# Splitting a weight conversion into two calls, reordering GpSimd's two operations on it, and finishing tiles one further ahead

## The chip, the core and the metric

The kernel runs on one core of one Trainium2 chip. The metric is device microseconds of one execution. TensorE (PE) does matmuls, VectorE (DVE), ScalarE (ACT) and GpSimd (POOL) do elementwise work, and SyncE's queue (SP) issues every DMA. Each engine works through its own instructions in the order in which they stand in the program.

## The reference

A retention layer over 4 batches, 8 heads, 768 positions and head size 64, followed by two feed-forward layers over 3072 tokens:

```
state = gamma * state + outer(k_t, v_t);  y_t = scale * q_t @ state
x = y as 3072 x 512
x = leaky_relu(x @ w1_in) @ w1_out            # 512 -> 2048 -> 512
x = h * sigmoid(1.702 h) @ w2_out, h = x @ w2_in
```

The four weights arrive as 64-bit floats, two 32-bit words for each element, and the kernel turns them into 32-bit floats by integer operations on the chip.

## The kernel before, in words

**Precision.** Each feed-forward product is made of three TensorE passes: an operand is split into a rounded part `hi` (ACT, L62) and a remainder `lo` (L63, on DVE, or on POOL for weights), and the passes are hi by lo, hi by hi, lo by hi, in this order. A weight tile of 128x512 thus needs `hi` for the first two matmuls of a group of 12 and `lo` from the third on.

**Converting a weight tile.** A weight has 16 tiles (index m). `load_raw` (L65) brings a raw tile (buffer "raw", 3 of them). `convert` (L70) does two ACT operations (L76 absolute value of the high word into tile "a", of which there are 2; L77 scaling of the low word), four DVE operations (L78, L79, L81 with one input, L83 with two) and one POOL addition (L85). `finish` (L88) then splits "a" into `hi` (ACT, L62) and `lo` (POOL, L63). For the second layer `finish_away` (L95) does the same and stores the result to DRAM, from where it is loaded again later.

**The schedule.** Three stages matter here; their names are used below.
- Stage A: 24 retention steps s (loop at L290 to L312). A step issues to PE the scores of s+1 (L200), the state and output matmuls of s (L231, L237, L243), then, on 15 of the steps 5 to 22 and on step 4, one group of 12 feed-forward matmuls `ffn_in(0, 0, m)` (L148). Steps 8, 13, 18 and 23 have no group. DVE does the masked scores "sm" (L204), the state "st" (L246) and "qs" (L211), POOL does "ks" (L215), SP loads the input of step s+4 into one of four buffers (L190).
- Stage B: the outer loop i = 16 to 25 at the end of the function. `out_of(n)` for n = 0 to 15 does the first block's output groups (L329, 12 matmuls each) and, between them, the input groups of the second block. Index i=16 has one output group, i=17 to 22 have two each, i=23 to 25 one each; each i has one input group before them. `out_of` issues the output group, then splits the activations of the group after next (`g_split`: ACT L62, DVE L63, into one of 2 tiles "g"), then calls `work()`.
- Stage C: everything after. `stage2` (L353) converts the second layer's weights there.

`work()` (L129) is called once for each tile of the first layer's 32: call n starts the load of tile n+2, converts tile n, and finishes tile n-1. The calls stand at steps 2, 3, 5, 6, 7, 8, 10, ... of stage A (L298), then once before the loop of stage B (L375) and once in each `out_of` of stage B. So the group for tile m is issued to PE right after the `work()` that finishes tile m (stage A), or in the `out_of` after it (stage B), and the POOL queue reads: addition of tile n, remainder of tile n-1.

Of the kernel before, what the change touches and what calls it, by code (L numbers as in the profile page):

```python
# [13 lines left out]
I32 = mybir.dt.int32  # L14
AF = mybir.ActivationFunctionType
ALU = mybir.AluOpType
# [8 lines left out]
KF = DFF // P  # L25
# [16 lines left out]
def retention_two_ffn(ctx: ExitStack, tc: tile.TileContext, qkv, consts, small, w1i, w1o, w2i, w2o, scratch, out):  # L42
    nc = tc.nc
# [14 lines left out]
    xf, raw, conv = {}, {}, {}  # L58
    wt = {}

    def split(hi, lo, src, eng=None):
        nc.scalar.copy(out=hi, in_=src)  # L62
        (eng or nc.vector).tensor_tensor(out=lo, in0=src, in1=hi.bitcast(F32), op=ALU.subtract)  # L63

    def load_raw(kind, m, src):  # L65
        t = cv_p.tile([P, 512, 2], U32, tag="raw", name="raw", bufs=3)
        nc.sync.dma_start(out=t, in_=src[m].bitcast(U32).rearrange("p (f two) -> p f two", two=2))
        raw[kind, m] = t

    def convert(kind, m):  # L70


        t = raw.pop((kind, m))
        low, high = t[:, :, 0], t[:, :, 1]
        a = cv_p.tile([P, 512], U32, tag="a", name="a")
        nc.scalar.activation(out=a.bitcast(F32), in_=high.bitcast(F32), func=AF.Abs)  # L76
        nc.scalar.activation(out=low.bitcast(I32), in_=low, func=AF.Copy, scale=2.0**-29)  # L77
        nc.vector.tensor_scalar(out=high, in0=high, scalar1=0x80000000, scalar2=None, op0=ALU.bitwise_and)  # L78
        nc.vector.tensor_scalar(out=a.bitcast(F32), in0=a.bitcast(F32), scalar1=HW_MIN, scalar2=HW_MAX,  # L79
                                op0=ALU.max, op1=ALU.min)  # L80
        nc.vector.tensor_scalar(out=a, in0=a, scalar1=3, scalar2=0x40000000,  # L81
                                op0=ALU.logical_shift_left, op1=ALU.bitwise_xor)
        nc.vector.scalar_tensor_tensor(out=a, in0=a, scalar=0x7FFFFFFF, in1=high,  # L83
                                       op0=ALU.bitwise_and, op1=ALU.bitwise_or)
        nc.gpsimd.tensor_tensor(out=a.bitcast(I32), in0=a.bitcast(I32), in1=low.bitcast(I32), op=ALU.add)  # L85
        conv[kind, m] = a, t

    def finish(kind, m, pool, eng):  # L88

        a = conv.pop((kind, m))[0].bitcast(F32)  # L90
        t = pool.tile([P, 2, 512], F32R, tag="w" + kind, name="w" + kind)
        split(t[:, 0], t[:, 1], a, eng)
        wt[kind, m] = t
# [26 lines left out]
    W0 = 4  # L120
    now_in = [[m for m in range(KF) if W0 + m * (N_STEPS - W0) // KF == s] for s in range(N_STEPS)]
# [3 lines left out]
    order = [("i", m) for m in range(KF)] + [("o", m) for m in range(KF)]  # L125
    pools = {"i": wi_p}
    done = [0]

    def work():  # L129

        n = done[0]
        done[0] += 1
        if n + 2 < len(order):
            kind, m = order[n + 2]
            load_raw(kind, m, w1i if kind == "i" else w1o)
        if n < len(order):
            convert(*order[n])
        if 0 < n <= len(order):
            kind, m = order[n - 1]
            finish(kind, m, pools[kind], nc.gpsimd)  # L140

    def ffn_in(lay, blk, m):
        h = ps.tile([P, TB], F32, tag="h", name="h")
        w = wt["i", m].rearrange("p s (k f) -> p s k f", k=NP)
        i = 0
        for k in range(NP):
            for a, c in ((0, 1), (0, 0), (1, 0)):
                nc.tensor.matmul(out=h, lhsT=w[:, a, k], rhs=xs[k][:, c], start=(i == 0), stop=(i == 3 * NP - 1))  # L148
                i += 1
        if m == KF - 1 and (lay, blk) != (1, NB - 1):  # L150
            x_split(lay * NB + blk + 1)
        t = h_p.tile([P, TB], F32, tag="h", name="h")
        if lay == 0:
            nc.scalar.activation(out=t, in_=h, func=AF.Lrelu)  # L154
        else:
            nc.scalar.activation(out=t, in_=h, func=AF.Sigmoid, scale=1.702)  # L156
            nc.vector.tensor_tensor(out=t, in0=h, in1=t, op=ALU.mult)  # L157
        hs[lay, blk, m] = t
# [3 lines left out]
    def g_split(key):  # L162
        gs[key] = g = g_p.tile([P, 2, TB], F32R, tag="g", name="g")
        split(g[:, 0], g[:, 1], hs.pop(key))


    with ExitStack() as actx:
# [24 lines left out]
        def a_scores(s):  # L192
            t = ins[s]
            qT = t[:, 0].rearrange("p (n i) -> p n i", n=NP)
            kT = t[:, 1].rearrange("p (n i) -> p n i", n=NP)
            ps = [ps_a.tile([P, NP, P], F32, tag=f"s{e}", name=f"s{e}") for e in range(2)]
            for n in range(NP):
                for e in range(2):
                    r = slice(D * e, D * e + D)
                    nc.tensor.matmul(out=ps[e][:, n], lhsT=kT[r, n], rhs=qT[r, n], start=True, stop=True,  # L200
                                     skip_group_check=True)
            sm = a_t.tile([P, 2, NP, P], F32, tag="sm", name="sm")
            for e in range(2):
                nc.vector.tensor_tensor(out=sm[:, e], in0=ps[e], in1=mask[:, :, e], op=ALU.mult)  # L204
            sc_t[s] = sm
# [13 lines left out]
        def a_out(s):  # L219
            b, c = steps[s]  # L220
            t = ins.pop(s)
            sm, ks, qs = sc_t.pop(s), ks_t.pop(s, None), qs_t.pop(s, None)
            v = t[:, 3].rearrange("p (n f) -> p n f", n=NP)
            if c < NC - 1:
                if c == 0:
                    kv_t[b] = ps_a.tile([P, NP, D], F32, tag="kv", name="kv", bufs=2)
                kv = kv_t[b]
                for n in range(NP):
                    for e in range(2):
                        r = slice(D * e, D * e + D)  # L230
                        nc.tensor.matmul(out=kv[r, n], lhsT=ks[:, 2 * n + e], rhs=v[:, n, r],  # L231
                                         start=(c == 0 and n == 0), stop=True, skip_group_check=True)
            o = ps_a.tile([P, NP, P], F32, tag="o", name="o", bufs=2)
            for n in range(NP):
                for e in range(2):
                    r = slice(D * e, D * e + D)
                    nc.tensor.matmul(out=o[r, n], lhsT=v[:, n, r], rhs=sm[:, e, n], start=(n == 0),  # L237
                                     stop=(c == 0), skip_group_check=True)
            if c > 0:
                for n in range(NP):  # L240
                    for e in range(2):
                        r = slice(D * e, D * e + D)
                        nc.tensor.matmul(out=o[r, n], lhsT=st[c % 2][r, n], rhs=qs[r, n], start=False, stop=True,  # L243
                                         skip_group_check=True)
            if c < NC - 1:
                nc.vector.tensor_tensor(out=st[(c + 1) % 2], in0=kv, op=ALU.mult,  # L246
                                        in1=gdec[:, c + 1, :].unsqueeze(2).to_broadcast([P, NP, D]))
            return o
# [34 lines left out]
        def keep_warm(n):  # L283

            for _ in range(n):
                nc.tensor.matmul(out=warm, lhsT=idle[:, :P], rhs=idle, start=True, stop=True, skip_group_check=True)
# [5 lines left out]
        for s in range(len(steps)):  # L292
            if s == 0:
                keep_warm(6)
            elif s + 1 < len(steps):
                a_scores(s + 1)
            o = a_out(s)
            if s >= W0 - 2 and done[0] < KF + 1 and (s < W0 or now_in[s - 1]):  # L298
                work()
            a_store(s, o)  # L300
            if s == 0:
                keep_warm(4)
                a_scores(1)
                keep_warm(6)
            if s + 2 < len(steps):
                a_decay(s + 2)
            if s + 4 < len(steps):
                a_load(s + 4)
            for m in now_in[s]:
                if m == KF - 1:  # L310
                    g_split(seq[0])
                ffn_in(0, 0, m)  # L312
# [37 lines left out]
    todo2 = [("i", m) for m in range(KF)] + [("o", m) for m in range(KF)]  # L350
    first2 = KF + LAG

    def stage2(i):  # L353
        n, late = divmod(i - first2, 2)
        if late:
            if n < len(todo2):
                convert(*todo2[n])
        else:
            if n < len(todo2):
                load_raw(*todo2[n], w2i if n < KF else w2o)  # L360
            if 0 < n <= len(todo2):
                finish_away(*todo2[n - 1])
# [9 lines left out]
            reload("o", m, wo_p)  # L372

    g_split(seq[1])
    work()  # L375
    n = 0
    for i in range(KF, len(seq)):
        lay, blk, m = seq[i]
# [77 lines left out]
```

## Time and profile before

| | |
|---|---|
| median of 3 runs | 1300.32 us (1300.06 to 1303.21) |
| profiled execution | 1301.17 us, of which the profile's span is 1299.0 us |
| busy over the span: PE, DVE, ACT, POOL | 1190.4, 441.3, 396.9, 190.7 us |
| stage A ends, stage B ends (us from the span's start) | 206.9, 359.4 |

The rows further down come from one execution, so sums are made against its span. "L148" is a line of the kernel. In a timeline row the first two numbers are start and duration in us; a bracket at the end tells how long the engine had been idle and what released it. A row whose count is above one stands for several instructions in a row, first start to last end.

### The profile page before, as it was taken

How to read it: one execution, taken by the hardware profiler on the slowest of the kernel's cores; microseconds unless marked ns; L12 is line 12 of the kernel's file. 1: busy time of each engine (PE TensorE's matmuls, PEld its weight loads, DVE VectorE, ACT ScalarE, POOL GpSimd, SP SyncE). 2: the span in 40 equal slices, each digit the busy share in tenths (PEclk: the TensorE clock that was granted, in tenths of full speed). 3: DMA queues.
4: the chain of work that ended last, by engine and by line, in shares of the span. 5: the costliest groups of instructions: out<-in, count | busy, mean ns of one | idle time of the engine just before them, and what ended most of it. 6: DMA issues, size and time to landing. Idle time of an engine off the chain costs nothing.

```text
span 1299.0 us, 14633 instructions
## 1 busy us (share of the span) xinstructions
PE 1190.4 (92%) x6040; PEld 964.8 (74%) x6040; DVE 441.3 (34%) x705; ACT 396.9 (31%) x671; POOL 190.7 (15%) x152
## 2 busy tenths in 40 slices
PE   8678777656699999999999999999999999999998
PEld 5566555434488888888888888888888888888887
DVE  6344343222234443443444222322323223223222
ACT  2222223222234443443444322222222222222222
POOL 3233232222212222222222000000000000000000
PEclk9898888777799999999999999999999999999999
DMA  9475542111033243332345633000000001000000
GB/s 365 159 255 189 180 144 98 49 48 51 14 97 130 99 141 118 130 130 97 130 178 202 214 136 113 33 1 33 33 8 27 32 33 33 1 33 1 1 33 33
DMA packets 36593, 123.39 MB, mean 95 GB/s; under 512 B 3760, under 2 KB 8880, under 8 KB 32432
## 3 DMA queue, kind: packets, MB, share of 16 engines
q1 hardware_dynamic: 36528, 122.47, 26.6%
q8 instruction: 47, 0.77, 0.3%
q14 instruction: 18, 0.15, 0.0%
HBM read 87.86 MB, written 34.60 MB: 94 GB/s over the span
## 4 chain that ended last, share of the span: by engine, by line
PE 86%; POOL 5%; DVE 4%; issue 3%; DMA 1%; ACT 1%; POOLq 0%; SPq 0%; ACTq 0%
PE h L148 41%; PE y L329 22%; PE y L331 20%; POOL a L85 2%; PE s L200 2%; POOL wo L63 1%; POOL wi L63 1%; DVE a L83 1%; DMA in<-qkv 1%; DVE a L81 1%; DVE sm L204 1%; PE o L237 1%; DVE raw L78 1%; PE o L243 1%; DVE a L79 1%
## 5 line engine op out<-in xcount | busy, mean ns | idle before, releaser
L148 PE MATMUL h<-xs,wi 128*128 128x512 f32 x2304 | 577.1, 400 | 44.2 <-POOL wi L63 44.2
L148 PEld LDWEIGHTS h<-xs,wi 128*128 128x128 f32 x2304 | 441.9, 193 | 145.5 <-POOL wi L63 50.7
L329 PE MATMUL y<-g,wo 128*128 128x512 f32 x1152 | 305.7, 416 | 56.3 <-POOL wo L63 42.2
L329 PEld LDWEIGHTS y<-g,wo 128*128 128x128 f32 x1152 | 231.4, 203 | 115.5 <-POOL wo L63 49.0
L63 DVE TENSOR_TENSOR g<-h,g 128x512 fp32r<-128x512 f32 x192 | 157.9, 823 | 468.0 <-ACT g L62 468.0
L331 PE MATMUL y<-wo,g 128*128 128x512 f32 x1152 | 275.1, 389 | 0.0
L331 PEld LDWEIGHTS y<-wo,g 128*128 128x128 f32 x1152 | 216.3, 188 | 44.9
L62 ACT CAST g<-h 128x512 fp32r<-128x512 f32 x192 | 119.4, 622 | 403.1 <-PE y L329 216.2
L85 POOL TENSOR_TENSOR a<-a,raw 128x512 int32<-128x512 int32 x64 | 87.6, 1369 | 447.2 <-DVE a L83 234.6
L154 ACT ACTIVATE h<-h 128x512 f32<-128x512 f32 x96 | 57.4, 598 | 236.3 <-PE h L148 236.3
L157 DVE TENSOR_TENSOR h<-h 128x512 f32<-128x512 f32 x96 | 66.4, 691 | 182.4 <-ACT h L156 182.4
L156 ACT ACTIVATE h<-h 128x512 f32<-128x512 f32 x96 | 57.4, 598 | 189.6 <-PE h L148 189.6
L204 DVE TENSOR_TENSOR sm<-s,cst 128x512 f32<-128x512 f32 x48 | 30.9, 684 | 103.5 <-PE s L200 98.4
L78 DVE TENSOR_SCALAR raw<-raw 128x512 uint32<-128x512 uint32 x64 | 27.2, 426 | 73.4 <-ACT a L76 73.4
L63 POOL TENSOR_TENSOR raw<-a,raw 128x512 fp32r<-128x512 f32 x32 | 41.2, 1287 | 61.4 <-ACT raw L62 61.4
L83 DVE SCALAR_TENSOR_TENSOR a<-a,raw 128x512 uint32<-128x512 uint32 x64 | 44.3, 692 | 2.2
L77 ACT ACTIVATE raw<-raw 128x512 int32<-128x512 uint32 x64 | 43.6, 681 | 0.0
L76 ACT ACTIVATE a<-raw 128x512 f32<-128x512 f32 x64 | 42.2, 659 | 0.7 <-DMA raw<-w2o 0.4
L200 PEld LDWEIGHTS s<-in 64*128 64x128 f32 x384 | 25.4, 199 | 10.5 <-issue 7.3
L63 DVE TENSOR_TENSOR xs<-x,xs 128x512 fp32r<-128x512 f32 x44 | 30.1, 693 | 4.5 <-ACT xs L62 4.5
L200 PE MATMUL s<-in 64*128 64x128 f32 x384 | 30.2, 296 | 1.2 <-DMA in<-qkv 1.2
L62 ACT CAST xs<-x 128x512 fp32r<-128x512 f32 x44 | 27.5, 624 | 7.0 <-PE h L148 4.7
(31 smaller groups left out, 353.3 us busy)
## 6 DMA issues: line engine op xcount, KB each, us to landing
in<-qkv SPq DMA_DIRECT2D x21, 1024.0 KB, 6.2
scratch<-raw SPq DMA_DIRECT2D x32, 512.0 KB, 2.9
x<-xd SPq DMA_DIRECT2D x11, 1024.0 KB, 4.8
raw<-w1i SPq DMA_DIRECT2D x16, 512.0 KB, 6.0
raw<-w1o SPq DMA_DIRECT2D x16, 512.0 KB, 3.3
raw<-w2i SPq DMA_DIRECT2D x16, 512.0 KB, 4.1
raw<-w2o SPq DMA_DIRECT2D x16, 512.0 KB, 4.3
wi<-scratch SPq DMA_DIRECT2D x16, 512.0 KB, 3.5
```

Source lines behind the costliest of these rows:

```text
L62: nc.scalar.copy(out=hi, in_=src)
L63: (eng or nc.vector).tensor_tensor(out=lo, in0=src, in1=hi.bitcast(F32), op=ALU.subtract)
L83: nc.vector.scalar_tensor_tensor(out=a, in0=a, scalar=0x7FFFFFFF, in1=high, op0=ALU.bitwise_and, op1=ALU.bitwise_or)
L85: nc.gpsimd.tensor_tensor(out=a.bitcast(I32), in0=a.bitcast(I32), in1=low.bitcast(I32), op=ALU.add)
L148: nc.tensor.matmul(out=h, lhsT=w[:, a, k], rhs=xs[k][:, c], start=(i == 0), stop=(i == 3 * NP - 1))
L154: nc.scalar.activation(out=t, in_=h, func=AF.Lrelu)
L156: nc.scalar.activation(out=t, in_=h, func=AF.Sigmoid, scale=1.702)
L157: nc.vector.tensor_tensor(out=t, in0=h, in1=t, op=ALU.mult)
L200: nc.tensor.matmul(out=ps[e][:, n], lhsT=kT[r, n], rhs=qT[r, n], start=True, stop=True, skip_group_check=True)
L204: nc.vector.tensor_tensor(out=sm[:, e], in0=ps[e], in1=mask[:, :, e], op=ALU.mult)
L329: nc.tensor.matmul(out=y[j], lhsT=w[:, a, cols], rhs=g[:, c], start=st_, stop=sp)
L331: nc.tensor.matmul(out=y[j], lhsT=g[:, a, cols], rhs=w[:, c], start=st_, stop=sp)
```

## The change

`convert` loses its last operation, the POOL addition, which becomes `round_in`. `work()` calls `round_in` of tile n after `finish` of tile n-1, so POOL's order is: remainder of tile n-1, addition of tile n. `stage2` calls `round_in` right after `convert`, so its order stays. The condition in stage A now holds at step 4 as well, which places every later call of stage A one tile further on, and a second `work()` stands ahead of stage B's loop, which does the same for the calls in `out_of`. Each tile is then finished one call earlier relative to the group that reads it.

```diff
         nc.vector.scalar_tensor_tensor(out=a, in0=a, scalar=0x7FFFFFFF, in1=high,
                                        op0=ALU.bitwise_and, op1=ALU.bitwise_or)
-        nc.gpsimd.tensor_tensor(out=a.bitcast(I32), in0=a.bitcast(I32), in1=low.bitcast(I32), op=ALU.add)
         conv[kind, m] = a, t
+
+    def round_in(kind, m):
+        a, t = conv[kind, m]
+        nc.gpsimd.tensor_tensor(out=a.bitcast(I32), in0=a.bitcast(I32), in1=t[:, :, 0].bitcast(I32), op=ALU.add)
...
         if 0 < n <= len(order):
             kind, m = order[n - 1]
             finish(kind, m, pools[kind], nc.gpsimd)
+        if n < len(order):
+            round_in(*order[n])
...
-            if s >= W0 - 2 and done[0] < KF + 1 and (s < W0 or now_in[s - 1]):
+            if s >= W0 - 2 and done[0] < KF + 1 and (s <= W0 or now_in[s - 1]):
                 work()
...
             if n < len(todo2):
                 convert(*todo2[n])
+                round_in(*todo2[n])
...
     g_split(seq[1])
+    work()
     work()
```

## Rows read from the trace of the kernel before

**Rows 1.** From the page: the TensorE clock granted in 40 equal slices of the span, in tenths of full speed, and the DMA rate in the same slices.
```profile
PEclk9898888777799999999999999999999999999999
...
GB/s 365 159 255 189 180 144 98 49 48 51 14 97 130 99 141 118 130 130 97 130 178 202 214 136 113 33 1 33 33 8 27 32 33 33 1 33 1 1 33 33
```

**Rows 2.** Who waited for whom in the first 480 us: total us, number of times, longest us.
```profile
PE h L148 <- POOL wi L63: 44.2, 14, 4.4
...
PE y L329 <- POOL wo L63: 42.2, 15, 2.9
```

**Rows 3.** One stretch of stage B by windows: length, busy us and instructions of PE, PEld, DVE, ACT and POOL, granted clock, DMA share, GB/s.
```profile
330.00:360.00 30.00, 20.25 (x64) 15.29 (x65) 6.95 (x15) 7.38 (x15) 7.48 (x6) 0.77 0.00 1
```

**Rows 4.** Timeline of one step of stage A that has a group.
```profile
103.61 0.60 ACT L62 CAST wi<-a 128x512 fp32r<-128x512 f32 x1
...
107.34 1.50 POOL L85 TENSOR_TENSOR a<-a,raw 128x512 int32<-128x512 int32 x1 [9.06 <-DVE a L83]
108.81 1.26 POOL L63 TENSOR_TENSOR wi<-a,wi 128x512 fp32r<-128x512 f32 x1
...
110.03 1.04 POOL L215 TENSOR_TENSOR ks<-in,smalls 128x512 f32<-128x512 f32 x1
110.12 4.03 PE L148 MATMUL h<-xs,wi 128*128 128x512 f32 x10 [4.37 <-POOL wi L63]
```

**Rows 5.** The chain that ended last, in order of time, over stage A: start, length, what ran. The first row is the start of step 5, the next two those of steps 8 and 9, the fourth that of step 10, the last two are the output matmuls of step 23.
```profile
34.47 1.14 PE s L200 x16
...
69.92 1.09 PE s L200 x16
...
73.52 1.09 PE s L200 x16
...
80.11 1.14 PE s L200 x16
...
204.12 1.70 PE o L237 x16
205.82 1.04 PE o L243 x16
```

**Rows 6.** Timeline of one `out_of` of stage B; the output group before it ended just ahead of the first row.
```profile
287.90 0.62 ACT L62 CAST g<-h 128x512 fp32r<-128x512 f32 x1 [6.82 <-PE y L329]
288.43 0.67 ACT L76 ACTIVATE a<-raw 128x512 f32<-128x512 f32 x1
288.56 0.69 DVE L63 TENSOR_TENSOR g<-h,g 128x512 fp32r<-128x512 f32 x1 [7.61 <-ACT g L62]
...
289.16 0.42 DVE L78 TENSOR_SCALAR raw<-raw 128x512 uint32<-128x512 uint32 x1
...
289.57 0.60 ACT L62 CAST wo<-a 128x512 fp32r<-128x512 f32 x1
...
290.42 0.69 DVE L83 SCALAR_TENSOR_TENSOR a<-a,raw 128x512 uint32<-128x512 uint32 x1
291.34 1.28 POOL L85 TENSOR_TENSOR a<-a,raw 128x512 int32<-128x512 int32 x1 [7.67 <-DVE a L83]
292.57 1.26 POOL L63 TENSOR_TENSOR wo<-a,wo 128x512 fp32r<-128x512 f32 x1
...
293.89 4.28 PE L329 MATMUL y<-g,wo 128*128 128x512 f32 x10 [2.90 <-POOL wo L63]
```

**Rows 7.** Timeline of the start of stage B: `hi` of the first output tile, and the ten matmuls of the first output group that need its `lo`.
```profile
209.05 0.61 ACT L62 CAST wo<-a 128x512 fp32r<-128x512 f32 x1
...
213.36 4.64 PE L329 MATMUL y<-g,wo 128*128 128x512 f32 x10 [2.92 <-POOL wo L63]
```

**Rows 8.** The chain that ended last, at the end of stage B: the first group after the 16th output group.
```profile
359.44 2.76 PE h L148 x12
```

**Rows 9.** Timeline of stage C: two groups of 12 in a row on PE, and a POOL addition with a DVE operation that starts behind it.
```profile
462.67 2.88 PE L148 MATMUL h<-xs,wi 128*128 128x512 f32 x12
...
463.42 1.30 POOL L85 TENSOR_TENSOR a<-a,raw 128x512 int32<-128x512 int32 x1 [6.23 <-DVE a L83]
463.53 1.74 DVE L63 TENSOR_TENSOR g<-h,g 128x512 fp32r<-128x512 f32 x1 [0.24 <-ACT g L62]
465.39 2.88 PE L329 MATMUL y<-g,wo 128*128 128x512 f32 x12
```

**Rows 10.** Timeline of stage A: a POOL addition with two DVE operations behind it that read PSUM and one SBUF tile (the two stand in one row).
```profile
118.98 1.53 POOL L85 TENSOR_TENSOR a<-a,raw 128x512 int32<-128x512 int32 x1 [7.91 <-DVE a L83]
...
119.27 1.28 DVE L204 TENSOR_TENSOR sm<-s,cst 128x512 f32<-128x512 f32 x2
```

**Rows 11.** All instructions of two DVE lines: durations in ns (least, median, most), first and last start in us.
```profile
L78 DVE TENSOR_SCALAR raw<-raw x64: 413/426/431, 21.4 to 711.6; 128x512 uint32<-128x512 uint32 x64
...
L246 DVE TENSOR_TENSOR st<-kv,smalls x20: 408/414/418, 12.1 to 195.1; 128x256 f32<-128x256 f32 x20
```

**Rows 12.** Loads of raw tiles, from issue to landing in us: least, median and most in the first 60 us, and the same from 60 to 365 us.
```profile
DMA to landing us min/median/max: 3.5/6.8/12.3
...
DMA to landing us min/median/max: 3.2/3.3/8.5
```

**Rows 13.** Two stretches of stage A by windows (columns as in rows 3): most of step 9, whose group found its tile finished, and the ten matmuls of a group after a wait.
```profile
73.50:77.10 3.60, 3.60 (x67) 3.14 (x65) 3.11 (x6) 0.59 (x1) 2.35 (x2) 1.00 0.76 291
...
97.30:102.00 4.70, 4.67 (x12) 3.25 (x12) 0.00 (x0) 0.00 (x0) 0.98 (x1) 0.50 0.79 303
```

## The prediction

> **What bounds the kernel now.** I began with the 40 slices [rows 1]: the granted clock of PE sags from the second slice to the eleventh, 11 x 32.5 = 357 us, and is 0.9 or more from there on. So only stages A and B are not bound by PE at its full speed. The waits of that stretch [rows 2] name the cause: PE's groups wait 14 times for a weight's `lo` in stage A and 15 times in stage B, 86.4 us in all. In stage B a window of 30 us holds 20.25 us of PE work at a clock of 0.77 [rows 3], and that work is itself stretched by the low clock, so more than the waits can be had back.
>
> The timelines show why `lo` is late. In stage B [rows 6] an output group ends at 287.9, then everything follows in one line: `g` on ACT, L76, the four DVE operations up to L83's end at 291.11, POOL's addition of tile n, and only then, at 292.57, the remainder of tile n-1 that PE needs. Its own input, `hi`, was there at 289.57 + 0.60 = 290.17. The remainder waits 2.4 us behind an addition that nobody needs yet. PE waits 2.90 us and then runs ten matmuls in about 4.2 us, the slow clock: a whole group takes 2.72 us in stage C (465.39 - 462.67) [rows 9]. In stage A [rows 4] it is the same: `hi` was there at 104.21, the remainder starts at 108.81, and PE waits 4.37 us.
>
> What a step costs with no such wait can be read off directly: step 9 has no `work()` ahead of its group, whose tile was finished in step 8. It takes 80.11 - 73.52 = 6.59 us, step 8 with no group 73.52 - 69.92 = 3.60 us [rows 5], and step 9 ran at a granted clock of 1.00 [rows 13], 2.4 GHz.
>
> **The change, part by part.** Counting the calls: `work()` number 2 moves from step 5 to step 4, 3 from 6 to 5, and so on to 16, from 22 to 21; number 18 moves ahead of stage B's loop. No instruction is added or removed; each tile's operations are called one step or one `out_of` earlier, and POOL's two swap.
>
> *Stage A.* From step 5 (34.47) to the end of step 23 (205.82 + 1.04 = 206.86) it takes 172.4 us. With `lo` finished a step ahead, the 15 steps with a group should take step 9's time and the three without step 8's: 15 x 6.59 + 3 x 3.60 = 109.7 us; step 23 keeps 206.86 - 204.12 = 2.74 us [rows 5]. That is 112.4 us: **60 us less**. In the new order the remainder starts about when its `hi` is ready, at 104.21 in the step shown [rows 4], and the group that reads it is issued a step later: some 6 us of cover. If that cover went (POOL held up for a whole step), each step would lose what the cover lacks. The moved load of a raw tile stands on SP ahead of the store and the input load of the same step. It waits for the addition of the tile three back, which ends about a step earlier; the input has some two and a half steps, 15 us, to land, so I cost it at nothing. The DMA rate it needs, 8.25 MiB in a period of five steps (5 inputs, 4 raw tiles, 5 half stores) of 30 us, is 288 GB/s; the first slice moved 365 [rows 1]. POOL's "ks", behind the addition, is wanted two steps on, and also costs nothing.
>
> *Stage B, the start.* `hi` of the first tile is ready at 209.66. Its addition was called in stage A, so the remainder starts about 0.1 us later and ends at 211.0, against 213.3 now [rows 7]; ten matmuls at 224 ns (2.72/12) end the first output group at 213.3.
>
> *Stage B, the rest.* 9 input and 15 output groups remain. Bound by PE they take 24 x 2.72 = 65.3 us and end at 278.6. Now they end at 359.44 [rows 8]: 80.8 us less. Whether the conversions keep up is the question. Two output groups and an input group, 8.16 us of PE, call `work()` twice. ACT has four operations in each (`g`, L76, L77, `hi`, about 0.57 us apart [rows 6]), 5.2 us for two with the input's activation: no bound. DVE and POOL now work at the same time, which they did not when POOL waited for DVE, and there rows show a conflict: L63 on DVE, 0.69 us alone [rows 6], took 1.74 us when it began 0.11 us behind a POOL addition of 1.30 us [rows 9], that is 1.19 us of waiting and 0.55 of work. They took turns. The masked scores, with one input in PSUM, ran their 0.64 each right through a POOL addition [rows 10]: no turns. L78, L79 and L81, with one input from SBUF, never met a POOL operation in this trace (L78 never took over 431 ns [rows 11]), so their price is unknown between two ends: no turns, or turns for their whole length. Nothing suggests a gain. I take turns: they move 512 elements in 0.42 us, where L246 takes 0.41 us for 256 [rows 11], so they use more of DVE's way to memory than an operation at the common pace, and the rows nearest in kind are those of DVE operations that read SBUF alone, which take turns.
>
> By that, one `work()` holds the common path for 1.23 (addition, start to start with the remainder) + 1.26 + 1.26 (L78 to L83, start to start) + 0.69 (L83) + 0.69 (`g`) = 5.13 us [rows 6], so two hold it 10.3 us, against PE's 8.16. For the six pairs of outputs (1 to 12) this costs up to 6 x 2.1 = 12.8 us; the tile finished ahead covers about one of these, so I take 12. The last three outputs have an input group each, 5.44 us of PE against 5.13. If the three one-input operations take no turns, two calls hold the path 7.7 us, below 8.16, and nothing is lost. Stage B then gives **69 us** (80.8 - 12), or 81.
>
> In stage A the same sum is 5 periods' worth of cover: four calls without `g` and five steps with "ks" (1.04 [rows 4]) and "qs" (as `g`) hold the path 4 x 4.44 + 5 x 1.73 = 26.4 us, against 4 x 6.59 + 3.60 = 30.0 us of PE. So it stays with PE.
>
> The Trainium skill (SBUF — State Buffer, "SBUF: two separate sides") says that VectorE and GpSimd share a pair of ports under an exclusive lock, for the length of an instruction, taken by VectorE's two-input operations and also by one-input operations in a two-port mode. By that rule the time is the one I forecast; by a reading of the trace alone that leaves one-input operations out it would be 12 us less. The row of the two-input case agrees (1.74 us behind 1.30); no run shows the one-input case.
>
> *Stage C* keeps its order, `round_in` standing where the addition stood, and PE is busy throughout: nothing.
>
> **Sum.** 60 + 69 = 129 us off a span of 1299.0 gives 1170; the profiled execution adds 2.2 and lies 0.85 above the median, so the median comes to about **1171 us**. 0.3%, or 4 us, is about what a measurement of this kernel can tell from no change.
>
> **The rivals.**
> 1. *No turns for one-input operations*: stage B bound by PE, 1171 - 12 = **1159 us**. For: PSUM readers pass freely [rows 10]. Against: their pace [rows 11].
> 2. *The clock stays low or a new wait appears.* Shorter waits may still end in half clock (1.2 GHz), as in the group of rows 13 at 0.50. Each of the 39 groups of both stages could cost up to 4.84 - 2.72 = 2.1 us (4.03/10 per matmul [rows 4]), 82 us in all: **1185 to 1253 us**. For: stage B by the forecast leaves PE idle 2.1 us in 10.3. Against: step 9, with no wait, had 1.00.
> 3. *Raw tiles come too late, and it ends slower.* Place: SP. The load of a tile waits until the addition three tiles earlier frees its buffer, and this addition now stands behind a remainder. From landing to the addition's end a conversion takes 292.6 - 288.4 = 4.2 us [rows 6], with the remainder ahead 5.5, so three conversions cannot take less than one landing plus 5.5 us. Now they take three times about 10.5 us (172.4 + 152.6 us for some 31). It decides against the change where landings exceed 26 us; at 30 us, 31 calls of 11.8 us give some 40 us more, **1340 us**. The longest landing was 12.3 us, at the start, the median later 3.3 [rows 12]. At 12.3 each call would still take only 5.9 us.
>
> **How the numbers follow.** Forecast 0.6, rival 1 0.22, rival 2 0.14, rival 3 0.03, and 0.01 for no change that can be seen. The predicted time is the forecast's, 1171. Its own range is 1163 to 1180. The range of 8 in 10 reaches down past rival 1's 1159 to 1155 and up into the mild part of rival 2, to 1190. Faster 0.96, same 0.01, slower 0.03.
>
> **What would show it.** Right: PE's waits for POOL's L63 nearly gone in stage A, steps with a group near 6.6 us, stage A's end near 147 us and stage B's about 84 us later, clock 1.00 in stage A, POOL's remainder ahead of its addition and L83 or L79 stretched by over 1 us where a remainder runs. Rival 1: L78 to L81 at 0.42 us inside a POOL operation, and no PE waits in stage B. Rival 2: clock under 0.9 in stage A or groups of 4 to 5 us. Rival 3: ACT's L76 waiting for DMA. I am wrong if stage A's steps stay above 8 us or if stage C moves by over 3 us.

## The result and the profile after

The changed kernel takes 1153.41 us (median of 4, 1153.35 to 1153.56) against 1300.59: ratio 0.8865, 95% interval 0.885 to 0.888, 147 us less. The forecast was 1171 with 1155 to 1190: the direction and the mechanism held, the gain was 18 us larger than the sum said, and the time lies just below the range.

Lines behind the edits have moved: L85 is now L89, L148 is L153, L329 is L334. The page after (first rows, and the granted clock in 40 slices of 28.8 us):

```profile
span 1151.2 us, 14612 instructions
...
PE 1139.5 (99%) x6039; PEld 936.2 (81%) x6040; DVE 485.2 (42%) x705; ACT 399.1 (35%) x671; POOL 203.1 (18%) x152
...
PEclk9999999999999999999999999999999999999999
```

The clock no longer sags [rows 1]. Two sums say where 147.8 us of span went. PE's idle time fell from 1299.0 - 1190.4 = 108.6 to 11.7 us, which is 96.9. Its busy time fell from 1190.4 to 1139.5, which is 50.9, with the same matmuls: that is work that ran at a lower clock before. Some 28.5 us of it lie in stage B and 22.5 in stage A, where the granted clock was 0.77 and 0.86 on the mean and is 1.00 now. So a third of the gain was never a wait.

The waits of PE, and of its weight loads (PEld), for a weight in the first 330 us, answering to [rows 2]; none is left in stage A:

```profile
PEld y L334 <- POOL wo L63: 7.0, 7, 1.1
...
PE y L334 <- POOL wo L63: 4.0, 7, 0.6
```

Stage A as the chain that ended last tells it (start, length, what ran), answering to [rows 5]. The group of step 4, then the starts of steps 5 to 9, and of step 10:

```profile
30.26 2.95 PE h L153 x12
33.21 1.09 PE s L205 x16
...
39.29 1.09 PE s L205 x16
...
44.83 1.09 PE s L205 x16
...
51.37 1.09 PE s L205 x16
...
54.98 1.09 PE s L205 x16
...
61.55 1.09 PE s L205 x16
```

By the differences of the starts, steps 5 to 9 take 6.08, 5.54, 6.54, 3.61 and 6.57 us. The last two are the 3.60 and 6.59 us that the forecast took from [rows 5]; steps 5 and 6 are shorter, and the forecast took 6.59 for them too.

Stage A's end and stage B's, by PE's timeline: the group of i=16, then the groups of i=25, n=15 and i=26.

```profile
139.82 3.02 PE L153 MATMUL h<-xs,wi 128*128 128x512 f32 x12
...
211.49 2.88 PE L153 MATMUL h<-xs,wi 128*128 128x512 f32 x12
214.21 2.88 PE L334 MATMUL y<-g,wo 128*128 128x512 f32 x12
216.93 2.88 PE L153 MATMUL h<-xs,wi 128*128 128x512 f32 x12
```

The same places before. These rows show a slip in what stands above: the 16th tile's remainder (L63, 360.69) comes after 359.44, so the group in [rows 8] follows the 15th output group, not the 16th, and stage B ended at 364.75, not 359.4:

```profile
359.27 2.92 PE L148 MATMUL h<-xs,wi 128*128 128x512 f32 x12
...
360.69 1.29 POOL L63 TENSOR_TENSOR wo<-a,wo 128x512 fp32r<-128x512 f32 x1 [5.45 <-ACT wo L62]
362.03 2.88 PE L329 MATMUL y<-g,wo 128*128 128x512 f32 x12
...
364.75 2.88 PE L148 MATMUL h<-xs,wi 128*128 128x512 f32 x12
```

With that the stages are, before and after: stage A from step 5 on 172.4 and 106.7 us, stage B 158.0 (206.77 to 364.75) and 77.1 us, stage C 934.3 and 934.3 us; the start is 1.3 us shorter.

One call of `work()` in stage B, answering to [rows 6] and to the question of turns:

```profile
161.89 2.56 PE L334 MATMUL y<-g,wo 128*128 128x512 f32 x10 [0.62 <-POOL wo L63]
162.31 0.68 DVE L63 TENSOR_TENSOR g<-h,g 128x512 fp32r<-128x512 f32 x1
...
162.47 1.69 POOL L89 TENSOR_TENSOR a<-a,raw 128x512 int32<-128x512 int32 x1 [0.62 <-DVE a L83]
162.91 1.53 DVE L78 TENSOR_SCALAR raw<-raw 128x512 uint32<-128x512 uint32 x1
...
164.36 0.41 DVE L79 TENSOR_SCALAR a<-a 128x512 f32<-128x512 f32 x1
...
164.81 0.43 DVE L81 TENSOR_SCALAR a<-a 128x512 uint32<-128x512 uint32 x1
164.89 1.49 POOL L63 TENSOR_TENSOR wo<-a,wo 128x512 fp32r<-128x512 f32 x1 [0.74 <-ACT wo L62]
165.27 1.66 DVE L83 SCALAR_TENSOR_TENSOR a<-a,raw 128x512 uint32<-128x512 uint32 x1
...
166.85 0.68 DVE L63 TENSOR_TENSOR g<-h,g 128x512 fp32r<-128x512 f32 x1
```

Follow the ends: `g` ends at 162.99; the addition, started at 162.47, ends at 164.16, 1.17 us later; L78, started in the middle of it, ends at 164.44, 0.28 behind it; L79 and L81 follow; the remainder ends 1.14 us behind L81, and L83 0.55 us behind the remainder. At any time one of the two engines gets on; the other's instruction stands or has not begun. L78, never above 0.431 us before [rows 11], takes 1.53: one-input operations do take turns. From `g` to `g` a call is 4.54 us, where DVE's five operations alone would take 2.6 and POOL's two 2.5. DVE counts as busy nearly throughout, though much of that is standing:

```profile
150.00:200.00 50.00, 46.63 (x200) 36.67 (x199) 49.25 (x56) 29.93 (x50) 34.99 (x23) 1.00 0.35 116
```

(Columns as in [rows 3].) PE needs 4.08 us for a call's share (three groups for two calls), so a pair is 9.08 instead of 8.16 us, and PE waits 0.62 us at one of the two groups (of the 0.92 us the profile counts only these as waiting).

### The profile page after: what moved, and what is told of

Its sections match the earlier page's. It is cut to its first block, busy times and chain, and to the rows that moved or that the text cites. A ratio compares the mean times of both kernels' runs of the same rounds, so it can differ in the third digit from the quotient of the medians.

```text
span 1151.2 us, 14612 instructions
## 1 busy us (share of the span) xinstructions
PE 1139.5 (99%) x6039; PEld 936.2 (81%) x6040; DVE 485.2 (42%) x705; ACT 399.1 (35%) x671; POOL 203.1 (18%) x152
## 4 chain that ended last, share of the span: by engine, by line
PE 89%; DVE 4%; issue 4%; POOL 2%; DMA 1%; SPq 0%; ACT 0%; POOLq 0%; DVEq 0%
PE h L153 42%; PE y L336 23%; PE y L334 20%; DVE raw L78 2%; PE s L205 1%; PE o L242 1%; PE o L248 1%; POOL a L89 1%; DVE a L83 1%; DMA cst<-consts 1%; DVE g L63 1%; PE kv L236 1%; POOL wi L63 1%; DVE a L81 0%; POOL ks L220 0%
## 5 line engine op out<-in xcount | busy, mean ns | idle before, releaser
L153 PE MATMUL h<-xs,wi 128*128 128x512 f32 x2304 | 555.7, 390 | 0.0
L153 PEld LDWEIGHTS h<-xs,wi 128*128 128x128 f32 x2304 | 431.1, 188 | 91.9 <-issue 2.8
L63 DVE TENSOR_TENSOR g<-h,g 128x512 fp32r<-128x512 f32 x192 | 157.6, 821 | 359.9 <-ACT g L62 359.9
L334 PE MATMUL y<-g,wo 128*128 128x512 f32 x1152 | 277.9, 390 | 4.0 <-POOL wo L63 4.0
L334 PEld LDWEIGHTS y<-g,wo 128*128 128x128 f32 x1152 | 215.6, 188 | 51.8 <-POOL wo L63 7.0
L89 POOL TENSOR_TENSOR a<-a,raw 128x512 int32<-128x512 int32 x64 | 95.2, 1487 | 255.6 <-DVE a L83 123.4
L78 DVE TENSOR_SCALAR raw<-raw 128x512 uint32<-128x512 uint32 x64 | 51.9, 811 | 73.4 <-ACT a L76 73.4
L83 DVE SCALAR_TENSOR_TENSOR a<-a,raw 128x512 uint32<-128x512 uint32 x64 | 58.8, 918 | 2.2
L63 POOL TENSOR_TENSOR raw<-a,raw 128x512 fp32r<-128x512 f32 x32 | 41.2, 1287 | 61.5 <-ACT raw L62 61.5
L76 ACT ACTIVATE a<-raw 128x512 f32<-128x512 f32 x64 | 42.5, 665 | 11.6 <-POOL wo L63 10.5
L79 DVE TENSOR_SCALAR a<-a 128x512 f32<-128x512 f32 x64 | 31.9, 498 | 0.0
L63 DVE TENSOR_TENSOR xs<-x,xs 128x512 fp32r<-128x512 f32 x44 | 29.8, 692 | 0.0
```

What stands on the lines that cost most here:

```text
L334: nc.tensor.matmul(out=y[j], lhsT=w[:, a, cols], rhs=g[:, c], start=st_, stop=sp)
```

## The experiments

**Which part brought the gain.** Four kernels undo one piece each.

`e1_order`: POOL's new order alone.
```diff
-            if s >= W0 - 2 and done[0] < KF + 1 and (s <= W0 or now_in[s - 1]):
+            if s >= W0 - 2 and done[0] < KF + 1 and (s < W0 or now_in[s - 1]):
...
     g_split(seq[1])
     work()
-    work()
```


> The changed order of POOL's two operations alone (remainder of tile n-1, then addition of tile n), with work() called where the kernel before calls it, so no tile is finished further ahead. Theory 1 (order and distance share the gain, order has most of it): in stage A the remainder ends at about the time PE reaches the third matmul (hi at 104.21 + 1.3 to 1.5 us, PE at 105.75), waits under 1 us, stage A within 8 us of the changed kernel's; in stage B the remainder ends 3.7 us or more behind an output group, so PE waits about 3 us in one of two and 0.5 to 1 us in the other, a pair of outputs takes 12 us or more: 1175 to 1195 us. Rival (the distance is what counts): waits stay at 3 us or more in stage A, time above 1250 us.

`e2_ahead`: the calls one tile further ahead alone.
```diff
             convert(*order[n])
+            round_in(*order[n])
         if 0 < n <= len(order):
             kind, m = order[n - 1]
             finish(kind, m, pools[kind], nc.gpsimd)
-        if n < len(order):
-            round_in(*order[n])
```


> The calls of work() one tile further ahead alone, with POOL's old order (addition of tile n, then remainder of tile n-1). Theory 1: stage A has no wait, since the remainder is read a step later; in stage B there is one input and one output group (5.4 us) between a call and the matmuls that read its tile, the remainder ends 6 to 7.3 us behind the call's output group, PE waits 0.2 to 1.5 us for each: 1154 to 1172 us. Rival (the order is what counts): 1250 us or more.

`e3_stage_a`: the changed kernel with the second half of e1's edit (no tile ahead in stage B).

> The changed kernel without the second work() ahead of stage B, so stage B has the new order but no tile ahead. Theory 1: stage A as in the changed kernel (ends near 139.8 us), stage B as in the order alone, pairs of 12 us or more: 1172 to 1190 us. Rival (one tile ahead is not needed once the order is changed): within 3 us of 1153.

`e4_stage_b`: the changed kernel with the first half of e1's edit (no tile ahead in stage A).

> The changed kernel without the call at step 4, so stage A has the new order but no tile ahead. Theory 1: PE's waits for the remainder in stage A are under 1 us each, 15 at most, stage B as in the changed kernel: 1154 to 1166 us. Rival (stage A needs the distance): waits of 3 us and half clock come back there, 1200 us or more.

Measured: e1 1188.74, e2 1172.16, e3 1186.73, e4 1157.30 us, beside 1300.74 for the kernel before. Order alone gives 112 us, distance alone 129, both 147: either takes most of the waits away, so the parts do not add up. The rivals of all four fall. In stage A the distance is worth only 4 us once the order is changed (e4 against 1153.4; its stage A takes 109.4 us against 106.7, its stage B 78.7 against 77.1), for the reason expected: PE's waits there with the order alone are 0.9 us in all,

```profile
PE h L153 <- POOL wi L63: 0.9, 2, 0.5
```

(e4's, of the first 330 us), against 44.2 [rows 2]. In stage B the distance is worth 33 us (e3 against 1153.4). e1's PE there, one pair:

```profile
172.91 0.74 PE L334 MATMUL y<-g,wo 128*128 128x512 f32 x2 [2.35 <-ACT wo L62]
...
174.26 4.64 PE L334 MATMUL y<-g,wo 128*128 128x512 f32 x10 [0.61 <-POOL wo L63]
...
187.60 5.98 PE L334 MATMUL y<-g,wo 128*128 128x512 f32 x12 [2.36 <-ACT wo L62]
```

A pair takes 14.7 us, with a wait for `hi` and then half clock: the ten matmuls at 174.26 ran at a granted clock of 0.50. The wait for `hi` is the part that [rows 2] did not show. The kernel before has it six times in stage B, and in e1 (second and third row) it is as long as before, while the wait for L63 has fallen from 42.2 us to 7.0:

```profile
PE y L329 <- ACT wo L62: 14.1, 6, 2.4
...
PE y L334 <- ACT wo L62: 14.1, 6, 2.4
PE y L334 <- POOL wo L63: 7.0, 13, 0.6
```

The order moves POOL's operations and cannot move ACT's `hi`. The distance does: the changed kernel has no such wait in stage B.

e2 missed its interval's upper end by 0.2 us; PE waits 15.3 us for L63 there, 12 times, up to 2.9 us, twice what I had expected at most. The trace shows what sets the pace. ACT's L76 waits for the remainder that frees one of the two tiles "a":

```profile
ACT a L76 <- POOL wo L63: 27.7, 14, 3.7
```

In the old order this closes a ring. In one call, L76 starts at 170.05, DVE's four operations end at 172.69, the addition starts at 172.93 and the remainder at 174.19, which ends at 175.93, and the next L76 starts at 175.96. So a call takes 5.9 us (5.4 to 6.0 in the other calls of stage B) against PE's 4.08. This is read from the trace; no run gives the old order a third tile "a".

**Half clock.** `e8_fill` adds work to the kernel before.
```diff
+    spare = ps_y.tile([P, 512], F32, tag="spare", name="spare")
...
             for i, (a, c) in enumerate(((0, 1), (0, 0), (1, 0))):
+                if (lay, blk, j, i) == (0, 0, 0, 2):
+                    for _ in range(8):
+                        nc.tensor.matmul(out=spare, lhsT=w[:, 0, cols], rhs=g[:, 0], start=True, stop=True)
```


> The kernel before, with eight extra matmuls (hi by hi into a PSUM tile that nobody reads) between the second and the third matmul of each of the 16 output groups of stage B, that is in the wait of 2.2 to 2.9 us; nothing else is changed. Eight take 8 x 0.224 = 1.8 us at full clock. Theory (PE's idle time also costs the clock behind it: 14 of the 15 groups shown behind a wait took 4.1 to 4.6 us for ten matmuls, one 2.56): the ten matmuls fall to 2.3 to 2.6 us, some 14 x 1.6 = 22 us less, 1272 to 1288 us. Rival (the slow groups have another cause than the idle time ahead of them): ten matmuls stay at 4.1 to 4.6 us, time 1297 us or more.

Measured: 1280.04 us (two runs, 1278.11 and 1281.96) against 1300.9, ratio 0.984 (0.982 to 0.986): 128 more matmuls, 20.9 us less. One group, to be compared with [rows 6]:

```profile
262.36 0.73 PE L334 MATMUL y<-g,wo 128*128 128x512 f32 x2 [2.35 <-ACT wo L62]
262.93 2.00 PE L331 MATMUL spare<-g,wo 128*128 128x512 f32 x8
266.06 2.57 PE L334 MATMUL y<-g,wo 128*128 128x512 f32 x10 [1.14 <-POOL wo L63]
```

Ten matmuls in 2.57 us instead of 4.28, though they start as late behind `g` as before (6.01 against 5.99 us). Of the 16 groups, 15 take 2.43 to 2.62 us for the ten and one 3.09. In three groups the eight extra matmuls themselves are slow (2.90, 3.48 and 3.40 us, not 2.00), each time behind the 2.36 us wait for `hi`, which was left empty. So the slow groups came from the idle time ahead of them, which shows, for stage B, where busy time could fall by tens of us without a matmul less. Not every such wait is followed by a slow group: in the kernel before, one of the 15 (at 224.02, after 2.23 us) took 2.56 us. Stage A's slow groups were not tested in this way; its windows show the same pattern [rows 13].

**What holds stage B now.** Theory 1: the turns of DVE and POOL. Rivals: the two tiles "a", the rate of calls not mattering, DVE's own busy time.

`e5_three_a`: a third tile "a".
```diff
-        a = cv_p.tile([P, 512], U32, tag="a", name="a")
+        a = cv_p.tile([P, 512], U32, tag="a", name="a", bufs=3)
```
(and, not shown, the savings named in the expectation: this kernel leaves out the 16th output tile)

> The changed kernel with three tiles a instead of two; to make room, stage A's store buffer has one tile instead of two and the 16th output tile of the first layer is the 15th again (its remainder and its reload are left out). In the changed kernel a pair of outputs takes 9.08 us in stage B and ACT's L76 waits for the remainder that frees its tile a, 10.5 us in all. Theory 1 (DVE and POOL take turns, and that sets the pair): the waits of L76 go, the pair stays at 8.9 to 9.1 us, time 1151 to 1156 us. Rival (the two tiles a set the pair): pair at PE's 8.16 to 8.5 us, time 1146 to 1150 us.

Measured 1152.84 us. The waits for a tile "a" are gone and the pair stays:

```profile
161.72 2.56 PE L340 MATMUL y<-g,wo 128*128 128x512 f32 x10 [0.63 <-POOL wo L63]
170.81 2.57 PE L340 MATMUL y<-g,wo 128*128 128x512 f32 x10 [0.63 <-POOL wo L63]
```

9.09 us. The tiles "a" are not it.

`e6_two_less`: two one-input operations less for each output tile.
```diff
-        nc.vector.tensor_scalar(out=a.bitcast(F32), in0=a.bitcast(F32), scalar1=HW_MIN, scalar2=HW_MAX,
-                                op0=ALU.max, op1=ALU.min)
-        nc.vector.tensor_scalar(out=a, in0=a, scalar1=3, scalar2=0x40000000,
-                                op0=ALU.logical_shift_left, op1=ALU.bitwise_xor)
+        if kind == "i" or done[0] > 2 * KF + 2:
+            nc.vector.tensor_scalar(out=a.bitcast(F32), in0=a.bitcast(F32), scalar1=HW_MIN, scalar2=HW_MAX,
+                                    op0=ALU.max, op1=ALU.min)
+            nc.vector.tensor_scalar(out=a, in0=a, scalar1=3, scalar2=0x40000000,
+                                    op0=ALU.logical_shift_left, op1=ALU.bitwise_xor)
```


> The changed kernel without L79 and L81 (the clamp, and the shift) for the first layer's output tiles, those converted in stage B and at its start; one call of work() then has 0.41 + 0.43 us less on DVE, 3.7 us instead of 4.54, below PE's 4.08. Theory 1 (turns): a pair falls from 9.08 to PE's 8.16 us, PE's waits in stage B go, time 1147 to 1149 us. Rival (the one-input operations cost nothing, the tiles a or ACT set the pair): pair stays above 8.8 us, 1152 to 1154 us.

Measured 1147.63 us. PE's waits for L63 in stage B fall from 4.0 to 0.6 us, and a pair takes PE's 8.16:

```profile
PE y L335 <- POOL wo L63: 0.6, 1, 0.6
...
148.96 5.60 PE L335 MATMUL y<-g,wo 128*128 128x512 f32 x24
...
157.12 5.60 PE L335 MATMUL y<-g,wo 128*128 128x512 f32 x24
```

Its stage B lasts 72.0 us (139.56 to 211.52) against the changed kernel's 77.1.

`e7_spread`: the same work, asked for more slowly.
```diff
-            if i < first2 and n > 2 * (i - KF):
+            if i < first2 + 6 and n > (3 * (i - KF) + 1) // 2:
```


> The changed kernel with stage B's outputs at three for two input groups instead of four (the condition becomes n > (3*(i-KF)+1)//2, up to six indices later). Three calls of work() then have 5 groups of 2.72 = 13.6 us of PE, 4.53 for each, what a call needs with turns. Theory 1: PE's waits in stage B fall from 4.0 us to under 1 us, and what a call was long by (0.46 us each for 12 calls, 5.4 us) comes back: 1147 to 1150 us. Rival (the loss in stage B is not set by the rate of calls): 1152 us or more.

Measured 1148.76 us, ratio 0.8828 (0.881 to 0.8846), with 0.9 us of such waits left. Nothing was made cheaper; the calls of `work()` only come at the pace they can be served at.

`e9_dve`: the remainder of output tiles on DVE.
```diff
-            finish(kind, m, pools[kind], nc.gpsimd)
+            finish(kind, m, pools[kind], nc.gpsimd if kind == "i" else nc.vector)
```


> The changed kernel with the remainder of the first layer's output tiles on DVE instead of POOL. POOL then holds the path 1.17 us in a call instead of 2.3, DVE 3.2 us instead of 2.2. Theory 1 (turns, the sum counts): 4.3 to 4.4 us for a call instead of 4.54, pair 8.6 to 8.8 us, 1150 to 1152.5 us. Rival (the engines' own busy time counts, not the sum): DVE has 0.69 us more in a call and is already busy throughout, so a call takes 5.2 us and the time rises to 1158 us or more.

Measured 1148.70 us, ratio 0.8828 (0.8813 to 0.8843), better than expected. The rival (busy time counts) falls; so does my figure for a call. The remainders on DVE:

```profile
159.71 0.69 DVE L63 TENSOR_TENSOR wo<-a,wo 128x512 fp32r<-128x512 f32 x1
...
163.90 0.68 DVE L63 TENSOR_TENSOR wo<-a,wo 128x512 fp32r<-128x512 f32 x1
...
168.09 0.69 DVE L63 TENSOR_TENSOR wo<-a,wo 128x512 fp32r<-128x512 f32 x1
```

4.19 and 4.19 us for a call, 8.4 for two and not 8.6 to 8.8. That is still a little above PE's 8.16, yet PE's pairs there take 8.16 and 8.19 us (starts at 157.59, 165.75 and 173.94) and it waits 0.8 us in all of stage B. That the tile finished ahead covers the difference is argued, not tested. A DVE with 0.69 us more to do gets through sooner, because a POOL operation of 1.14 us has left the turns.

`e10_both`: e7 and e9 together.

> The spread outputs (three for two inputs) and the output tiles' remainder on DVE together. Either alone took nearly all of PE's waits out of stage B (0.8 and 0.9 us left). Theory (stage B is then bound by PE, so the two do not add up): 1148.0 to 1149.0 us, no change against either alone beyond 0.7 us. Rival (each removed another half of the loss): 1144 us or less.

Measured 1147.95 us, ratio 0.8827 (0.8815 to 0.8839): the gains do not add up and the rival falls. The time lies 0.05 us below the expected interval, and 0.75 and 0.81 us below e9 and e7 where at most 0.7 was expected. PE is busy for the whole of a long stretch of its stage B:

```profile
150.00:215.00 65.00, 65.00 (x289) 53.81 (x288) 46.85 (x81) 36.14 (x64) 20.03 (x13) 1.00 0.29 101
```

So stage B is then bound by PE. This version, like e7 and e9, is 4.7 to 5.5 us below the changed kernel; the 0.8 us between it and those two was not measured side by side and is not explained.

## Why the prediction was wrong by 18 us

The steps that held: the cause (a remainder behind an addition), the swap and the distance taking PE's waits away, step 9 as the pattern of a step with no wait, the clock at 1.00, stage C unmoved, and turns for one-input operations, which rival 1 denied. Rivals 2 and 3 did not come: no group at half clock, and L76 waited for a load once, for 0.4 us.

Four terms of the sum, each of them a saving, were too small. Together they are 1.3 + 5.7 + 5.3 + 6.7 = 19.0 us of span, against 1170 - 1151.2 = 18.8; the rest is rounding.

- **Stage A's steps, 5.7 us.** The sum gave all 15 steps step 9's 6.59 us. But the first chunk of a batch has no second output matmul (L248, 1.02 us, missing in step 6) and the last no state matmul (L236, missing in step 5): 5.54 and 6.08 us. This stands in the code (`if c > 0`, `if c < NC - 1`), and one measured step was taken for all; the six steps concerned make 4.7 us. Step 23 was kept at its 2.74 us and takes 2.05, because its first output matmuls had run slow (L237, 1.70 us in [rows 5]). Measured 106.7 us against 112.4.
- **The start, 1.3 us.** Step 4's group had a wait too (0.96 us for L63), which the sum left out.
- **Stage B's old end, 5.3 us.** It was read one pair of groups too early (359.44 for 364.75, shown above), so what it takes now was set against too short a past. [rows 8] was taken for the group behind the 16th output group without counting tiles.
- **The price of turns, 6.7 us.** This is the step to learn from. The turns are real, and the sum charged each operation its duration when alone: 5.13 us for a call. Measured: 4.54 us. The row that proved the turns already had the right figure: in [rows 9] L63 on DVE took 1.74 us, "1.19 us of waiting and 0.55 of work", and I then charged 0.69. An operation that has stood waiting needs less than its duration once the other engine is done. From end to end in the call above: addition 1.17 (charged 1.23), L78 to L81 1.08 (1.26), remainder 1.14 (1.26), L83 0.55 (0.69), `g` 0.60 (0.69), which makes the 0.59 us. So the pair was 9.08 and not 10.3 us, and turns cost stage B 77.1 - 71.8 = 5.3 us and not 12 (71.8 is the start's 6.5 and 24 groups of 2.72, and e6's stage B took 72.0). That turns cost anything at all is shown by e6, e7 and e9, each of which reaches about 1148 us in its own way. Stage B bound by PE, which rival 1 expected, is that 1148 us, 5 us below what the change reached; its figure of 1159 held the first three slips too.

The range was at fault with them: its lower end, 1155, was rival 1 less 4 us, and so allowed for unknown prices but not for a miscount in what was known.

Two figures of the working were slips that moved nothing: a matmul of 2.72/12 us is 227 ns, not 224, and 6 x 2.1 is 12.6, not 12.8.

## What to carry to other kernels

When an in-order engine alternates between "prepare the next" and "finish the last", put the finishing first and make one more tile ahead: either took most of the wait here, and what was left of each was covered by the other. Count what a wait costs twice, as time and as the slow matmuls behind it. And where two engines take turns, charge a waiting operation what it takes after the other has ended, read from a row where it did wait, and check the stages' ends by counting tiles, not by the look of the chain.

## What the runs showed of the hardware

- DVE operations with one input from SBUF at the fast pace (L78 0.42 us alone) stand while POOL works, as the two-input ones do: 1.53 us behind an addition. In stage A of the changed kernel L79 and L81 reach 1.51 and 1.40 us where a remainder runs on POOL (0.42 and 0.43 alone). The Trainium skill (SBUF — State Buffer, "SBUF: two separate sides") describes this as an exclusive lock on a shared pair of ports; the trace now agrees for both kinds.
- POOL's instructions stand in the same way: an addition of 1.30 us alone takes 1.69 when it starts 0.16 us into a DVE operation of 0.68.
- Filling PE's waits of 2.2 to 2.9 us in stage B with matmuls for nothing made a kernel 20.9 us faster: the ten matmuls behind one took 2.57 instead of 4.28 us.
